# Pooled attention and a GELU MLP on one core: the loads of one group's K and V issued behind a transpose

## The chip, the cores and the metric

The kernel runs on 1 core of one Trainium2 chip. The metric is the device time of one execution in microseconds (us), and the figure quoted is the median of several runs. The profile comes from one execution that the hardware profiler recorded. Its span runs from the first to the last instruction on the core, so it is a little shorter than the time of the run.

The engines are called as in the profile: PE is the matrix engine (PEld its weight loads), DVE the vector engine, ACT the scalar engine, POOL the GpSimd engine. SP is the engine that issues every load, store and transposing DMA of this kernel, in program order.

## The reference

Attention over 8 batches and 8 heads, with 576 queries of 64 elements each. K and V are first averaged over 8 neighbouring rows, so that 72 pooled keys remain per head. An MLP with a tanh GELU follows on the 4608 tokens.

```python
k_p = k.reshape(B, H, S // 8, 8, D).mean(axis=3)      # B, H, S, D = 8, 8, 576, 64
v_p = v.reshape(B, H, S // 8, 8, D).mean(axis=3)
scores = q @ k_p.transpose(0, 1, 3, 2) / np.sqrt(D)
attn = np.exp(scores - scores.max(-1, keepdims=True))
attn = attn / (attn.sum(-1, keepdims=True) + 1e-09)
x = (attn @ v_p).transpose(0, 2, 1, 3).reshape(B * S, H * D)      # 4608 x 512
h = x @ w_in                                                     # w_in 512 x 2048
g = 0.5 * h * (1 + np.tanh(np.sqrt(2 / np.pi) * (h + 0.044715 * h ** 3)))
out = g @ w_out                                                  # w_out 2048 x 512
```

## The kernel before

**Groups and steps.** The tokens are worked on in nine groups of 512. Groups 0 to 7 hold the first 512 queries of each batch; the ninth, called `R`, gathers the last 64 queries of all eight batches. The order is 0 to 6, then `R`, then 7. Each step is the MLP of one group, with the attention of the next group woven into it, and the loads for the group after that. Step 0 is `mlp_first`. The loop from line 727 makes the steps 1 to 8; in step 1 (`n_ == 1`) the MLP is that of group 1, the attention that of group 2 (`n`), and the loads are those of group 3 (`n2`).

**The order by hand.** The schedule is manual: every engine runs its instructions in program order. PE's matmuls of the MLP are counted by slots. The first 64 slots are the hidden layer (`hidden`, line 376: four matmuls for each of 16 rows of blocks, then a GELU on ACT). Slots 64 to 175 are the output layer (line 485: seven products, 16 matmuls each, of which three take sums that `g_sums` makes on DVE). `at(hooks, s, f, ...)` puts the call `f` ahead of the matmul of slot `s`; calls of one slot run in the order of the `at` lines.

**What the slots of step 1 hold.** These matter here:

- Slot 22: `pool`, `dup_k` and `k_transpose_dma` of group 2. DVE averages K, and SP issues the transposing DMA into `kTd` (line 199).
- Slots 28, 32, 36, 40: `cast_q` of group 2 on ACT (line 88), a quarter of the queries each, from `q_sb` into the bf16 tile `q_b`.
- Slot 28 too: `load_kv` of group 3 (lines 667 to 674): a new `kv` tile, then four loads. Those of line 108 carry 1024 KB each (K first and V last), and those of lines 103 and 101 carry 128 KB each.
- Slot 41: `q_transpose_dma` of group 2 (line 220). SP waits for the four casts, then issues one transposing DMA from `q_b` into `qT`.
- Slots 57 and 58: `load_q` of group 3 (line 120, 1024 KB) and two parts of `R`'s queries (line 124, 128 KB each).
- Slots 68, 71, 92 and 100: `scores` on PE (line 229), which reads `qT` and `kbd`, then the exponential on ACT (line 244).
- Slots 81, 97, 104 and 114: `norm` (lines 251, 260, 263) and `e_transpose_dma` (line 293), which SP issues into `eT`.
- Slot 116: `cast_gated`, POOL's cast of group 3's queries.
- Slot 156: the first half of `values_part` (line 348) on PE, which reads the first two of the four `eT` parts. The second half follows in slot 4 of the next step and reads the other two.
- Slot 164: `q_transpose_dma` of group 3.

The later steps have the same slots with two differences: their query transposes were issued in the step before (slot 164), and `pool` and `k_transpose_dma` come in slot 12.

**Buffers.** `kv` and `q_sb` have two buffers each; `qT`, `q_b`, `kTd` and `eT` have one. The `kv` tile of group 3 takes the buffer of group 1, whose last reader on DVE ends at 49.2 us in the profiled run.

Of the kernel before, what the change touches and what calls it, by code (L numbers as in the profile page):

```python
# [19 lines left out]
def kernel(  # L20
# [655 lines left out]
    def at(hooks, s, f, *a):  # L676
        hooks.setdefault(s, []).append(lambda: f(*a))
# [6 lines left out]
    hooks = {}  # L684
# [42 lines left out]
    for n_, g in enumerate(seq):  # L727
        if n_ == 0:
            continue
        hooks = {}  # L730
        if n_ == 1:
            for i in range(1, 4):
                at(hooks, i, w_sums, i, 0, NP, nc.vector)
            at(hooks, 36, g_sums, 0, 4)
        else:
            at(hooks, 20, g_sums, 0, 2)
            at(hooks, 36, g_sums, 2, 4)
        at(hooks, 57, g_sums, 4, 6)
        at(hooks, 65, g_sums, 6, 8)
        if n_ + 1 < len(seq):  # L740
            n = seq[n_ + 1]
            b = B - 1 if n == R else n
            kv = n != B - 1
            if n_ == 1:
                for j in range(4):
                    at(hooks, 28 + 4 * j, cast_q, n, j, j + 1, nc.scalar)
                at(hooks, 41, qT_tile, n)
                at(hooks, 41, q_transpose_dma, n)
            if kv:
                t0 = 22 if n_ == 1 else 12  # L750
                at(hooks, t0, pool, b, 0, 5)
                at(hooks, t0, dup_k, b, 0, 5)
                at(hooks, t0, kT_tile, b, None)
                at(hooks, t0, k_transpose_dma, b)
                t1 = t0 + (16 if n_ == 1 else 24)
                at(hooks, t1, pool, b, 5, 9)
                at(hooks, t1, spread_v, b, nc.gpsimd)
                at(hooks, 56, k_spread, b, [nc.vector, nc.vector])
            for j in range(4):
                sj = 64 + ([4, 4, 30, 34] if n == R else [4, 7, 28, 36])[j]  # L760
                at(hooks, sj, scores, n, j)
                at(hooks, sj, exps, n, j)
                if j == 0:
                    at(hooks, 64 + 17, eT_tile, n)
                nj = 64 + [17, 33, 40, 50][j]
                at(hooks, nj, norm, n, j, nc.gpsimd if j == 1 else nc.vector)
                at(hooks, nj, e_transpose_dma, n, j)
            at(hooks, 64 + 66, nc.scalar.preload_act_table_set, GELU_SET)
            at(hooks, 64 + 92, xT_tile, n)
            at(hooks, 64 + 92, values_part, n, 0, [nc.scalar, nc.vector])  # L770
        if n_ > 1:
            at(hooks, 4, values_part, g, 1, [nc.scalar, nc.vector])
        if n_ + 2 < len(seq):
            n2 = seq[n_ + 2]
            if n2 != R:
                at(hooks, 57, q_tile, n2)
                at(hooks, 57, load_q, n2, 0, 4, nc.sync)
            at(hooks, 64 + 52, cast_gated, n2)
            at(hooks, 64 + 100, qT_tile, n2)
            at(hooks, 64 + 100, q_transpose_dma, n2)  # L780
            at(hooks, 28, load_kv, n2)
        if n_ == 1:
            at(hooks, 58, q_tile, R)
        if 1 <= n_ <= 4:
            at(hooks, 58, load_q, R, n_ - 1, n_, nc.sync)
        mlp(g, hooks, n_ + 1 == len(seq), n_ > 1)
# [30 lines left out]
```

## Time and profile before

| What | Value |
|---|---|
| median of 6 runs | 296.47 us (295.70 to 298.62) |
| the profiled run | 295.7 us |
| its span | 294.0 us |
| PE busy | 279.3 us (95%) |
| DVE, ACT, POOL busy | 206.4, 166.8, 63.6 us |
| DMA | 56.41 MB, mean 192 GB/s |
| mean granted PE clock | 0.987 of full speed |

How to read it: the page gives the busy time of each engine, the span in 40 equal slices (7.35 us each) with a digit for the busy tenths, and the groups of instructions with the idle time ahead of them and what ended it. The chain of waits follows the work that ended last back to the start. The timeline of SP lists its issues with the time that each issue held SP; the time from an issue to the landing of its data is given separately.

### The profile page before, as it was taken

The page shows a single profiled execution, that of the slowest core. Times are in us where ns is not written, and L with a number is a line of the kernel's source. Part 1 is how long each engine was busy: PE and PEld are TensorE (multiplying, and loading weights), DVE is VectorE, ACT ScalarE, POOL GpSimd, SP SyncE. Part 2 cuts the span into 40 slices and gives each one's busy share as a digit, 9 for nine tenths or more (in the row PEclk, how much of TensorE's full clock was granted, in tenths as well). Part 3 has the DMA queues.
Part 4 walks back from the last instruction along what each step waited for, and adds up shares of the span by engine and source line. Part 5 has one row for each costly group of instructions (what it writes and reads, how often), then busy time and mean ns, then how long its engine had stood idle before and what let it go on. Part 6 is the DMA issues. An engine that isn't in the chain of part 4 may idle for free.

```text
span 294.0 us, 5594 instructions
## 1 busy us (share of the span) xinstructions
PE 279.3 (95%) x2203; PEld 199.5 (68%) x2203; DVE 206.4 (70%) x379; ACT 166.8 (57%) x262; POOL 63.6 (22%) x97
## 2 busy tenths in 40 slices
PE   8799999991999999999999999999999999999994
PEld 4578753440887488748874886498648965986583
DVE  4891879985476897689768967895899435944531
ACT  1586584792345674666367636664675467546610
POOL 3575343021040124022302220312031200100000
PEclk9999999998699999999999999999999999999999
DMA  7999999999647797799888949824841560144003
GB/s 230 354 387 337 377 383 183 337 293 312 176 90 214 227 298 91 215 236 294 86 221 256 278 89 223 290 57 110 197 141 26 120 162 2 28 99 108 1 2 144
DMA packets 71419, 56.41 MB, mean 192 GB/s; under 512 B 45664, under 2 KB 55392, under 8 KB 71392
## 3 DMA queue, kind: packets, MB, share of 16 engines
q1 hardware_dynamic: 71392, 56.04, 70.6%
q8 instruction: 17, 0.28, 0.4%
q14 instruction: 10, 0.08, 0.1%
HBM read 36.70 MB, written 9.44 MB: 157 GB/s over the span
## 4 chain that ended last, share of the span: by engine, by line
PE 80%; DMA 11%; DVE 5%; SPq 1%; POOL 1%; issue 0%; DVEq 0%
PE mm L485 31%; PE mm L380 28%; PE mm L391 9%; DMA kv<-in_k_dram 5%; DMA qT<-q_b 4%; PE xo L348 4%; DMA q_sb<-in_q_dram 3%; PE sc L229 2%; PE x L485 2%; DVE eb L263 1%; PE mm L396 1%; DVE kv L147 1%; DVE den L251 1%; DVE kv L148 1%; SPq L108 1%; PE xo L356 1%
## 5 line engine op out<-in xcount | busy, mean ns | idle before, releaser
L380 PE MATMUL mm<-xT,w_in_b 128*128 128x512 bf16 x400 | 87.8, 379 | 0.0
L382 ACT ACTIVATE gT<-mm 128x512 bf16<-128x512 f32 x100 | 59.7, 598 | 25.0 <-PE mm L380 24.9
L380 PEld LDWEIGHTS <-w_in_b 128*128 128x128 bf16 x400 | 39.1, 98 | 45.8 <-issue 0.3
L485 PEld LDWEIGHTS <-gT 128*128 128x128 bf16 x512 | 50.3, 100 | 7.9
L169 POOL TENSOR_TENSOR vbd<-kvb,vmask 128x256 bf16<-128x256 bf16 (+2 forms) x40 | 23.7, 614 | 95.3 <-DVE kvb L149 95.1
L391 PE MATMUL mm<-xT,w_in_b 128*128 128x256 bf16 x352 | 42.2, 273 | 0.2 <-DVE xT L90 0.2
L485 PEld LDWEIGHTS <-stage 128*128 128x128 bf16 x384 | 37.2, 98 | 4.2
L391 PEld LDWEIGHTS <-w_in_b 128*128 128x128 bf16 x352 | 34.0, 98 | 4.2 <-issue 0.3
L393 ACT ACTIVATE gT<-mm 128x512 bf16<-128x512 f32 x44 | 26.2, 597 | 15.6 <-PE mm L391 15.6
L244 ACT ACTIVATE e<-sc 128x576 f32<-128x576 f32 x36 | 22.6, 650 | 19.1 <-PE sc L229 11.1
L485 PE MATMUL mm<-w_out_b,gT 128*128 128x256 bf16 x240 | 32.6, 283 | 0.0
L90 DVE CAST xT<-xo 128x512 bf16<-128x512 f32 x16 | 11.0, 691 | 29.0 <-PE xo L348 24.1
L485 PE MATMUL mm<-tw,gT 128*128 128x256 bf16 x240 | 28.7, 273 | 0.0
L88 ACT COPY osb<-mm 128x512 f32<-128x512 f32 x23 | 13.5, 586 | 26.6 <-PE mm L485 26.6
L251 DVE TENSOR_REDUCE den<-e 128x8 f32<-128x576 f32 x36 | 26.4, 735 | 2.3 <-ACT e L244 2.3
L485 PE MATMUL mm<-tw,stage 128*128 128x256 bf16 x224 | 27.9, 273 | 0.0
L147 DVE TENSOR_TENSOR kv<-kv 128x1024 f32<-128x1024 f32 (+3 forms) x19 | 21.0, 1107 | 7.6 <-DMA kv<-in_k_dram 6.3
L431 DVE TENSOR_TENSOR stage<-gT 128x512 bf16<-128x512 bf16 (+1 forms) x31 | 16.2, 522 | 13.1 <-ACT gT L382 7.8
L88 ACT CAST xT<-xo 128x512 bf16<-128x512 f32 (+1 forms) x18 | 11.3, 633 | 18.4 <-PE xo L348 11.0
L263 DVE TENSOR_TENSOR eb<-e,r 128x576 bf16<-128x576 f32 x24 | 20.3, 847 | 0.8
L229 PE MATMUL sc<-kbd,qT 128*128 128x144 bf16 x128 | 13.8, 232 | 6.9 <-DMA qT<-q_b 6.6
L263 POOL TENSOR_TENSOR eb<-e,r 128x576 bf16<-128x576 f32 x6 | 6.9, 1149 | 60.3 <-ACT e L244 54.5
(86 smaller groups left out, 303.7 us busy)
## 6 DMA issues: line engine op xcount, KB each, us to landing
kv<-in_k_dram SPq DMA_DIRECT2D x7, 1024.0 KB, 6.6
q_sb<-in_q_dram SPq DMA_DIRECT2D x7, 1024.0 KB, 10.6
out_dram<-osb SPq DMA_DIRECT2D x13, 512.0 KB, 3.0
kv<-in_v_dram SPq DMA_DIRECT2D x6, 1024.0 KB, 8.6
kv<-in_v_dram SPq DMA_DIRECT2D x4, 512.0 KB, 10.3
w_in_s<-in_moe_w_in_dram SPq DMA_DIRECT2D x4, 512.0 KB, 9.0
stage<-in_moe_w_in_dram SPq DMA_DIRECT2D x4, 512.0 KB, 11.5
w_out_s<-in_moe_w_out_dram SPq DMA_DIRECT2D x2, 1024.0 KB, 13.4
```

Source lines behind the costliest of these rows:

```text
L88: eng.copy(out=out, in_=in_)
L147: add(out=t[:, :, 0:4, :], in0=t[:, :, 0:4, :], in1=t[:, :, 4:8, :], op=ALU.add)
L169: eng.tensor_tensor(out=vbd[p0:128, b, n0:n1, :].rearrange("p (c r) (hh d) -> p c (r hh) d", c=max(m, 1), d=D), in0=kvb[p0:128, 4 + c0:4 + ...
L229: nc.tensor.matmul(out=o, lhsT=qT[:, j, pr, :], rhs=kbd[:, g, pr].rearrange("d hh s -> d (hh s)"), start=True, stop=True)
L244: nc.scalar.activation(out=e.rearrange("p (x h) s -> p x (h s)", x=2), in_=sc[:, :, 0:4 * Sp], func=ACT.Exp, scale=1.0 / 64.0)
L251: nc.vector.reduce_sum(out=den, in_=e, axis=AX.X)
L263: eng.tensor_tensor(out=o.rearrange("p (h s) -> p h s", s=Sp), in0=e, in1=r.unsqueeze(2).to_broadcast([128, H, Sp]), op=ALU.mult)
L380: nc.tensor.matmul(out=hp, lhsT=w_in_b[:, ko, fo * 128:(fo + 1) * 128], rhs=st[g]["xT"][:, ko, :], start=(i == 0), stop=(i == KO - 1))
L382: nc.scalar.activation(out=gT[:, fo, :], in_=hp, func=ACT.Gelu_apprx_tanh)
L391: nc.tensor.matmul(out=hp[:, f, :], lhsT=w_in_b[:, ko, (fo + f) * 128:(fo + f + 1) * 128], rhs=st[g]["xT"][:, ko, c0:c0 + 256], start=(ko ...
L393: nc.scalar.activation(out=gT[:, fo:fo + 2, c0:c0 + 256], in_=hp, func=ACT.Gelu_apprx_tanh)
L485: nc.tensor.matmul(out=xs[p] if acc is xs else acc[:, p, :], lhsT=lt, rhs=rt, start=bool(fresh and m == 0 and (p == 0 or (last and acc is ...
```

## The change

One number: in step 1 alone, `load_kv` is put in slot 44 in place of slot 28. Its four loads are issued after `q_transpose_dma` of slot 41 instead of before it. In the other steps `load_kv` stays in slot 28.

```diff
@@ -778,7 +778,7 @@
             at(hooks, 64 + 52, cast_gated, n2)
             at(hooks, 64 + 100, qT_tile, n2)
             at(hooks, 64 + 100, q_transpose_dma, n2)
-            at(hooks, 28, load_kv, n2)
+            at(hooks, 44 if n_ == 1 else 28, load_kv, n2)
         if n_ == 1:
             at(hooks, 58, q_tile, R)
         if 1 <= n_ <= 4:
```

## The prediction

> **What bounds the kernel now.** First the page: PE is busy in nine tenths or more of nearly every slice, so only PE's gaps and its clock can be won. Slices 10 and 11 (66.2 to 80.8 us) have a low clock, and line 229 (`scores`) waited 6.6 us for one transfer.
>
> ```profile
> PE   8799999991999999999999999999999999999994
> PEclk9999999998699999999999999999999999999999
> L229 PE MATMUL sc<-kbd,qT 128*128 128x144 bf16 x128 | 13.8, 232 | 6.9 <-DMA qT<-q_b 6.6
> ```
>
> Second, the chain of waits in order of time, around that place and in the next step.
>
> ```profile
> 52.64 10.41 PE mm L380 x48
> 63.05 10.55 DMA qT<-q_b
> 73.61 0.05 issue
> 73.66 0.66 PE sc L229 x4
> ...
> 86.59 0.87 PE xo L348 x8
> ...
> 104.81 0.25 PE sc L229 x4
> ...
> 115.42 0.87 PE xo L348 x8
> ```
>
> PE stands still from 67.04 us (73.66 less 6.62) to 73.66. From the first scores to `values_part` step 1 then takes 86.59 − 73.66 = 12.93 us; step 2 takes 115.42 − 104.81 = 10.61 us for the same matmuls. The 2.32 us between them is the slow clock. So the place holds 6.62 + 2.32 = 8.94 us.
>
> Third, SP's timeline (start, time that SP was held, line): why is `qT` late?
>
> ```profile
> 59.11 1.23 SPq L199 DMA_TRANSPOSE kTd<-kvb  x1
> 60.40 0.73 SPq L108 DMA_DIRECT2D kv<-in_k_dram  x1
> ...
> 62.36 0.59 SPq L108 DMA_DIRECT2D kv<-in_v_dram  x1
> 63.05 8.54 SPq L220 DMA_TRANSPOSE qT<-q_b  x1
> 71.64 0.58 SPq L120 DMA_DIRECT2D q_sb<-in_q_dram  x1
> ...
> 89.32 3.24 SPq L220 DMA_TRANSPOSE qT<-q_b  x1
> ```
>
> Group 3's K and V were issued just ahead of it. V landed 9.5 us after its issue, at 71.9; `qT` took 10.55 us and landed at 73.6. The six other `qT` transposes landed 5.0 (three times), 5.3, 5.9 and 6.8 us after their issue, and held SP for 3.0 to 3.8 us, not 8.54.
>
> Fourth, windows of the same stretch (the last three columns are clock, DMA share and GB/s).
>
> ```profile
> 63.00:64.00 1.00, 1.00 (x6) 0.47 (x5) 0.97 (x2) 0.96 (x2) 0.00 (x0) 1.00 0.90 62
> 64.00:65.00 1.00, 1.00 (x7) 0.47 (x5) 0.93 (x2) 0.69 (x2) 0.00 (x0) 1.00 0.84 207
> 70.80:71.40 0.60, 0.00 (x0) 0.00 (x0) 0.00 (x0) 0.00 (x0) 0.00 (x0) 0.92 1.02 315
> 73.20:73.80 0.60, 0.14 (x2) 0.15 (x3) 0.00 (x0) 0.00 (x0) 0.00 (x0) 0.50 0.47 85
> 78.00:78.60 0.60, 0.60 (x6) 0.54 (x5) 0.60 (x2) 0.00 (x0) 0.00 (x0) 0.89 0.26 43
> 78.60:79.20 0.60, 0.60 (x10) 0.56 (x9) 0.53 (x3) 0.00 (x0) 0.00 (x0) 1.00 0.00 0
> ```
>
> They cut the traffic into parts. `kTd` (landed at 65.3) takes the low rate up to about 64.3. K and V move from 64.3 to 71.3 (7.0 us), `qT` to 73.5 (2.2 us), the query loads to 78.1 (some 4.5 us). The DMA is then idle until SP issues the first `eT` at 79.84.
>
> **The change, part by part.**
>
> *Issue of `qT`.* SP waits for the last cast, which ends on ACT at 62.34 + 0.64 = 62.98 us. Before, SP was through with V at 62.95; so the issue stays at 63.05. It now holds SP for about 3.2 us (3.0 to 3.8 in the undisturbed rows) instead of 8.54. Nothing else is behind it on SP but loads.
>
> *Landing of `qT`.* Only `kTd` is ahead, busy to 64.3. Undisturbed landings of 5.0 to 6.8 us give 68.05 to 69.85. I take 5.5, a little over their mean because of `kTd`: 68.55. PE needs it at 67.04, so the scores start at 68.6 and 1.6 us of the stall stay; 5.1 us go.
>
> *The clock.* The row: idle from 67.04, the clock fell at about 71.3 (0.92 in 70.8 to 71.4), 4.3 us on, and was back at 78.1. [...]
>
> *The four loads.* They are issued from about 66.35 instead of 60.40 and held SP for 2.4 us together: until 68.9, and the query loads follow at once (before: 71.64). Their data come behind `qT`'s, from about 68.4. [...] For K and V themselves it costs nothing: DVE first reads group 3's K at 92.04, and 68.4 + 7.0 = 75.4 is far ahead, even with that read some 5 us earlier. [...] The cost lies with the transfers behind them.
>
> *What is late next: `eT`.* Loads of 3.67 MB (2 × 1024, 2 × 128, 1024 and 2 × 128 KB) are in front of the `eT` transposes. They took 7.0 + 4.5 = 11.5 us in step 1; in step 2 they moved from about 98.2 to 109.0 (10.8). With 11.2, they end at 68.4 + 11.2 = 79.6 instead of 78.1. But `values_part` now wants the first two `eT` at 68.6 + 10.61 = 79.2 instead of 86.59. That is a new stall. For its size nothing in the trace fits exactly, so two ends. If both `eT` (5 blocks each) already stand in the queue, they need 10/16 of `qT`'s 2.2 us and 0.3 us to land: 79.6 + 1.7 = 81.3. If SP is held until the loads have moved, as `qT` held it until 71.59, then the first issue ends at 79.9, the second takes 1.2 us and lands 1.4 us after its issue (the undisturbed 2.6 less 1.2): 82.5. I take the middle, 81.9: a stall of 2.7 us, too short for the clock.
>
> *Behind it.* The third and fourth `eT` take 2 × 1.25 us of issue after the second, and the second half of `values_part` comes 3.06 us after the first (89.65 − 86.59): just in time. Group 3's queries land near 80, and POOL's cast, 84.40 before and gated by the fourth `norm`, comes at about 79.5 to 80. Its query transpose follows at 84 to 85 and is wanted at about 100. From there every step is as before: step 1's `values_part` to step 2's is 28.83 us, step 2's to step 3's 144.25 − 115.42 = 28.83.
>
> **Sum.** `values_part` of step 1 starts at 81.9 + 0.1 = 82.0 instead of 86.59: 4.6 us less. In terms: −5.1 of stall, −2.3 of clock, +2.8 of the new wait. The profiled run of 295.7 becomes 291.1. It is the fastest of six; set against the median, 296.47 − 4.6 = 291.9 us.
>
> **Rivals.** A change of 0.5% (1.5 us) is about what the measurement can tell from none.
>
> *The new wait doesn't arise* (10%). The `eT` transposes find a gap, or the loads move at the 390 GB/s of their best windows: 3.67/0.39 = 9.4 us, end at 77.8. With `qT` after 5.0 us the gain is 8.94 − 1.1 = 7.8: 288.7 us. For it: the DMA idled before `eT` in the run before. Against: 390 GB/s was never held for 3.67 MB; 10.8 us is the best seen.
>
> *The new wait is long* (12%). `qT` at 69.85, loads from 69.6 in 11.5 us, `eT` held and its landing stretched by 1 us (the first `eT` of steps 2 to 4 took 4.4, 3.6 and 4.2 us): 81.1 + 2.9 + 1 = 85.0. Gain 1.5 without a fall of the clock, none or −0.8 with it: 295 to 297.
>
> *Slower* (4%). One mechanism: K and V, then the queries, crawl in front of `eT` with scores, exponentials and PE back at full load. At 68 to 69 us, K and V moved at 236 GB/s. Were all 3.67 MB that slow, 15.6 us, they would end at 84.0 and the second `eT` land at 86.9, 7.7 us after it is wanted; the clock falls too (2.3): 86.9 − 86.59 + 2.3 = 2.6 slower, 299.1 us. It decides from a landing at about 84.3 on with the clock fallen (85.8 for a loss over 1.5 us). Against: the same loads took 10.8 us in step 2 with PE at full load.
>
> *It doesn't do what it says* (2%). `qT` was slow through stores and `kTd` ahead, not through K and V: 296.5 us. The stores of step 0 landed by 65.0 and `kTd` at 65.3, which leaves 8.3 us to V and `qT`.
>
> **How the numbers follow.** The forecast has 72%; within it `qT`'s 5.0 to 6.8 us and the two ends for `eT` give gains of about 3 to 6: 290.5 to 293.5. The range reaches to the rivals on both sides, 289.2 to 294.6. Faster by over 0.5%: 72 + 10 and half of the long wait, 88%. Within 0.5%: 7%. Slower: 5%.
>
> **What would show it.** In the new profile: the `qT` issue of 63.05 holds SP for 3 to 4 us and lands at 68 to 70; the wait of line 229 is 1 to 3 us; the clock stays at 1.00 from 66 to 80; K is issued at about 66.4; a new wait of line 348 for `eT` of 1.5 to 4 us at about 79 to 82; all later steps are 28.8 us. I am wrong if line 348 waits over 4 us, if the clock falls there, or if `qT` lands after 70.

## The result and the profile after

The changed kernel takes 295.12 us (median of 34 runs, 293.45 to 296.62) against 296.52 us of the kernel before in all its runs (71, 294.79 to 298.62). The ratio is 0.9958, with a 95% interval of 0.9944 to 0.9971: 0.4% faster, 1.4 us where 4.6 were forecast. The profiled run took 295.35 us with a span of 293.6 us.

First the page of the changed kernel. The rows of the two waits have changed places.

```profile
PE   8879999999669999999999999999999999999994
PEclk9999999999959999999999999999999999999999
L348 PE MATMUL xo<-eT,vbd 128*128 128x256 bf16 x96 | 13.3, 284 | 5.2 <-DMA eT<-eb 5.2
```

Line 229 no longer stands among the costly groups with a wait for `qT`; line 348 now waits 5.2 us for `eT`. The low clock has moved from slices 10 and 11 to slice 12. Next, the changed kernel's chain of waits in order of time (start, us, what).

```profile
63.02 4.30 DMA qT<-q_b
67.32 0.05 issue
67.37 0.42 PE sc L229 x4
...
72.04 4.82 PE mm L485 x44
76.86 1.94 SPq L293
...
78.90 4.29 DMA eT<-eb
83.19 0.14 issue
83.33 1.87 PE xo L348 x8
85.19 4.11 PE mm L485 x20
...
93.66 10.36 PE mm L380 x48
```

PE waits for the second of the four `eT` parts, since line 348 reads the first two. `qT` lands 4.3 us after its issue instead of 10.55, and the scores start at 67.37 instead of 73.66: 6.3 us earlier. Then PE stands still from 78.16 to 83.33. After that the 8 matmuls of line 348 take 1.87 us (0.87 before) and the 20 behind them 4.11 us (2.18 before): the clock is halved (0.50 in a row of the windows below). From the first `values_part` to the 48 matmuls of step 2's hidden layer (line 380) it is 93.66 − 83.33 = 10.33 us, before 94.02 − 86.59 = 7.43. The new wait thus costs 5.17 us and 2.9 us of clock, and of the 6.3 + 2.3 = 8.6 us that were won only 94.02 − 93.66 = 0.36 us are left in this pair of profiles: 0.2 us went into the first scores (0.42 us in place of 0.25). The profiled run of the kernel before was 0.8 us faster than its median, so the pair shows less than the medians do. The steps from 2 on are 28.83 us, as before.

SP's timeline of the changed kernel shows why `eT` is late (start, time SP was held, line):

```profile
63.02 2.45 SPq L220 DMA_TRANSPOSE qT<-q_b  x1
65.52 0.58 SPq L108 DMA_DIRECT2D kv<-in_k_dram  x1
...
67.37 0.59 SPq L108 DMA_DIRECT2D kv<-in_v_dram  x1
68.00 0.64 SPq L120 DMA_DIRECT2D q_sb<-in_q_dram  x1
68.68 4.93 SPq L124 DMA_DIRECT2D q_r<-in_q_dram  x2
73.72 9.39 SPq L293 DMA_TRANSPOSE eT<-eb  x4
```

The four `eT` hold SP for 9.39 us (5.99 before). The first alone holds it for 5.08 us and lands 8.4 us after its issue; the second is issued at 78.90 and lands 4.3 us later, at 83.2. Half-microsecond windows of the same run (the last three columns are clock, DMA share and GB/s; a share can exceed 1, because a packet's whole time is counted in the window in which it begins):

```profile
77.50:78.00 0.50, 0.50 (x6) 0.34 (x4) 0.50 (x2) 0.00 (x0) 0.00 (x0) 1.00 1.25 288
79.50:80.00 0.50, 0.00 (x0) 0.00 (x0) 0.00 (x0) 0.00 (x0) 0.00 (x0) 1.00 1.77 58
80.50:81.00 0.50, 0.00 (x0) 0.00 (x0) 0.00 (x0) 0.00 (x0) 0.28 (x1) 1.00 0.08 16
81.50:82.00 0.50, 0.00 (x0) 0.00 (x0) 0.00 (x0) 0.00 (x0) 0.50 (x2) 1.00 1.28 283
82.00:82.50 0.50, 0.00 (x0) 0.00 (x0) 0.00 (x0) 0.00 (x0) 0.50 (x1) 0.67 1.26 284
83.50:84.00 0.50, 0.50 (x4) 0.38 (x3) 0.00 (x0) 0.00 (x0) 0.00 (x0) 0.50 0.94 180
```

From 79.5 almost nothing moves for 2 us (58 GB/s in 79.5 to 80.0, 16 in 80.5 to 81.0), and only from 81.5 do the `eT` data come (283 GB/s). In 82.0 to 82.5 the clock falls (0.67 on average, 0.50 behind it). The loads in front are not through when the rate drops. Group 3's queries land at 80.6, where POOL's cast of them can start, and the two loads of `R`'s queries, issued at 68.7 and 71.9, take 12.3 and 9.6 us and land at 81.0 and 81.5 (a row of POOL's timeline, then two of the view of `q_r`):

```profile
80.72 2.02 POOL L90 CAST q_b<-q_sb 128x1024 bf16<-128x1024 f32 x2 [3.40 <-DMA q_sb<-in_q_dram]
L124 SPq DMA_DIRECT2D q_r<-in_q_dram x2: 1712/2442/3172, 68.7 to 71.9; - x2
DMA to landing us min/median/max: 9.6/11.0/12.3
```

### The profile page after: what moved, and what is told of

It reads as the page before. It is cut to its first block, busy times and chain, and to the rows that moved or that the text cites. A ratio compares the mean times of both kernels' runs of the same rounds, so it can differ in the third digit from the quotient of the medians.

```text
span 293.6 us, 5594 instructions
## 1 busy us (share of the span) xinstructions
PE 280.0 (95%) x2203; PEld 199.8 (68%) x2203; DVE 207.0 (71%) x379; ACT 166.7 (57%) x262; POOL 63.0 (21%) x97
## 4 chain that ended last, share of the span: by engine, by line
PE 87%; DVE 7%; DMA 3%; SPq 1%; issue 0%; POOL 0%; ACT 0%; POOLq 0%
PE mm L485 31%; PE mm L380 28%; PE mm L391 12%; PE xo L348 4%; PE x L485 2%; PE sc L229 2%; PE warm L591 2%; DVE den L251 2%; DMA qT<-q_b 1%; DMA eT<-eb 1%; DVE eb L263 1%; PE mm L396 1%; PE vp L156 1%; SPq L293 1%; PE xo L356 1%; DVE kv L147 1%
## 5 line engine op out<-in xcount | busy, mean ns | idle before, releaser
L485 PE MATMUL mm<-w_out_b,gT 128*128 128x256 bf16 x240 | 30.8, 273 | 0.0
L485 PE MATMUL mm<-tw,gT 128*128 128x256 bf16 x240 | 30.2, 282 | 0.0
L432 DVE TENSOR_TENSOR gT<-gT 128x512 bf16<-128x512 bf16 (+1 forms) x31 | 14.8, 477 | 6.6 <-ACT gT L382 5.1
L348 PE MATMUL xo<-eT,vbd 128*128 128x256 bf16 x96 | 13.3, 284 | 5.2 <-DMA eT<-eb 5.2
```

The source lines that it names most:

```text
L348: nc.tensor.matmul(out=xo[pr // 2][:, x, :], lhsT=vbd[:, g, n, :], rhs=eT[:, 2 * half:2 * half + 2, c, :], start=(y == 0), stop=(y == 1))
L485: nc.tensor.matmul(out=xs[p] if acc is xs else acc[:, p, :], lhsT=lt, rhs=rt, start=bool(fresh and m == 0 and (p == 0 or (last and acc is ...
```

## The experiments

Each is an edit of the changed kernel, save where it says otherwise. The ratios are to the kernel before, run on the same chip. They are what to compare: the experiments ran on three chips, and the kernel before has medians of 295.38 to 296.83 us there.

**1. K and V behind `eT`.**

```diff
-            at(hooks, 44 if n_ == 1 else 28, load_kv, n2)
+            at(hooks, 115 if n_ == 1 else 28, load_kv, n2)
```

> In step 1 load_kv goes to slot 115, behind the four eT transposes, in place of slot 44. Theory (the gain was given back because the eT transposes stand behind 3.67 MB of loads, and the wait of 5.2 us then halves the clock for another 2.9 us): line 348 no longer waits for eT in step 1, the clock stays full after 60 us, and the time falls by about 8 us from the changed kernel's 295.1, to 287. Rival (the loads cannot be hidden anywhere near there): K and V come too late for step 2 or hold up group 3's query transpose behind them, a new wait of line 229 or line 147 takes the place, and the time stays at 292 or more.

Measured: 291.31 us, ratio 0.984 (0.978 to 0.990). In step 1 there was no wait for `eT`, as the theory has it. But 287 was missed: step 2 got a wait of line 348 for `eT` of 1.8 us. The rival was right that the wait moves, and wrong about the line. DVE pools K and the 128 KB piece of V (line 101) at the start of step 2, and they were there only at 85.5. So `kTd` and the loads behind it came late as measured from PE, and in the chain of this run stands:

```profile
79.69 5.80 DMA kv<-in_v_dram
85.61 1.50 DVE kv L147
...
104.84 4.72 DMA eT<-eb
```

**2. The query loads behind `eT`.** The `at` lines of slots 57 and 58 get `115 if n_ == 1 else ...`.

> load_kv stays in slot 44; the query loads of step 1 (group 3's and R's first part, 1.3 MB) go from slots 57 and 58 to slot 115, behind the eT transposes. Theory (the amount of data ahead of eT sets the new wait): only K and V are ahead, 7 us of data from about 68, so the second eT lands at 77.5 to 78.7 where PE wants it at 78.2; the wait is 0 to 0.5 us, no fall of the clock, time 287 to 288. Rival (a transposing DMA behind any running load starts some 2 to 3 us late): the second eT lands at 79.5 to 80.5, a wait of 1.3 to 2.3 us without a fall of the clock, time 288.5 to 289.5.

Measured: 291.30 us, ratio 0.987 (0.981 to 0.992). Step 1 again has no wait. The chain of this run shows where the gain went; 78.08 is step 1's `values_part`, the rest is step 2.

```profile
78.08 0.87 PE xo L348 x8
...
96.31 0.25 PE sc L229 x4
...
104.85 4.94 DMA eT<-eb
109.79 0.09 issue
109.88 1.03 PE xo L348 x8
```

Step 2 takes 109.88 − 78.08 = 31.8 us instead of 28.8. SP's timeline of this run says why: the transpose of group 3's queries had to wait for queries loaded late, and it held up everything behind it.

```profile
88.05 1.81 SPq L220 DMA_TRANSPOSE qT<-q_b  x1
...
91.18 1.45 SPq L199 DMA_TRANSPOSE kTd<-kvb  x1
92.67 0.65 SPq L108 DMA_DIRECT2D kv<-in_k_dram  x1
```

Step 2's K was issued 96.31 − 92.67 = 3.6 us ahead of its scores; before, it was 104.81 − 96.49 = 8.3 us. The loads were late relative to PE here too; in step 1 of the changed kernel K is issued 67.37 − 65.52 = 1.85 us ahead of the scores.

**3. Only R's part behind `eT`.** The two loads of 128 KB go from slot 58 to slot 115.

> Only R's first part (two loads of 128 KB in rows of 256 bytes) goes behind the eT transposes; K, V and group 3's queries stay ahead of them. In the changed kernel the DMA moved 16 to 71 GB/s between 80 and 81.5 us, after the loads had slowed and before the eT data came. Theory of bytes: 0.26 MB less at 290 GB/s is 0.9 us; eT's second part lands at 82.3, the wait is 4.3 us, the clock may still fall; time 292 to 294.5. Theory of small pieces (the pause comes from the tail of the short-row loads): the pause goes, the second eT lands near 80, the wait is under 2 us, the clock stays full; time 288 to 289.5.

Measured: 291.69 us, ratio 0.986 (0.981 to 0.991). Neither theory holds as it stood. The chain:

```profile
74.72 6.52 DMA eT<-eb
81.24 0.14 issue
81.37 1.87 PE xo L348 x8
83.24 2.82 PE mm L485 x20
```

The second `eT` landed at 81.2, 2.0 us earlier, which is twice what the bytes explain. The stretch with almost no traffic stayed (36 GB/s or less from 78.5 to 79.5), so it does not come from R's part alone. The wait was 3.2 us, and that still halved the clock (0.50), for 3.4 us.

**4. Keep PE busy in the wait.**

```diff
+            if n_ == 1:
+                at(hooks, 64 + 92, warm_up, 20, "sc")
             at(hooks, 64 + 92, values_part, n, 0, [nc.scalar, nc.vector])
```

> The changed kernel with 20 matmuls of zeros (128x512) put into PE's program of step 1 just ahead of slot 156's values_part; they take 20 x 0.216 = 4.3 us of the 5.2 us in which PE waits for eT, and nothing reads them. Theory (2.9 us of what was given back are the clock, halved by the idle wait): the clock stays at 1.00 from 66 to 95 us and the time falls to about 292.2. Rival (the clock's fall costs little, or falls all the same): 295, or more if the matmuls come on top of the wait.

Measured: 292.55 us, ratio 0.989 (0.985 to 0.994), which lies apart from the changed kernel's interval. The second `eT` came as late as ever (83.4), but the clock stayed (mean 1.000 in the profiled run):

```profile
79.04 4.34 DMA eT<-eb
83.38 0.14 issue
83.51 1.03 PE xo L348 x8
84.55 2.18 PE mm L485 x20
```

The same matmuls take 1.03 and 2.18 us in place of 1.87 and 4.11. The fall of the clock is worth 1.9 us by the ratios (0.9958 less 0.9893) and 2.6 by the medians (which are not of the same chips); the profile has 2.9.

**5 and 6. V behind `eT`; then also R's parts one step later.**

```diff
+            if n_ == 1:
+                at(hooks, 115, load_main, n2, "v", 0, 4, nc.sync)   # load_kv(3) in slot 44 without it
...
-        if 1 <= n_ <= 4:                                            # only in the sixth
-            at(hooks, 58, load_q, R, n_ - 1, n_, nc.sync)
+        if 2 <= n_ <= 5:
+            at(hooks, 58, load_q, R, n_ - 2, n_ - 1, nc.sync)
```

> The changed kernel, but group 3's V load of 1024 KB goes from slot 44 to slot 115, behind the eT transposes; K and the two halves stay in slot 44. Theory (the data ahead of eT set the wait): 1.05 MB at 300 GB/s less is 3.5 us; the second eT lands near 79.7 instead of 83.2, PE wants it at 78.1, a wait of 1 to 2 us, the clock stays full; 295.1 less 3.5 less 2.9 is 288.7, say 288 to 290. Rival (any load that is moved back only moves the wait): step 2 gets a new wait for its eT of 2 us or more, as the two runs before it had, and the time is 291 or more.

> As the run before, and R's four parts are loaded in steps 2 to 5 instead of 1 to 4 (0.26 MB less ahead of eT in step 1). Theory: the second eT lands another 1 to 2 us earlier, at 78 to 78.7, a wait under 0.6 us in step 1, the time 1 us under the run before: 287 to 289. Rival (the wait comes back in step 2, whose loads are untouched): no better than the run before.

Measured: 289.66 us, ratio 0.976 (0.973 to 0.980), and 288.23 us, ratio 0.971 (0.968 to 0.974). In the fifth run the second `eT` landed at 80.9, later than the 79.7 expected, with a wait of 2.7 us that left the clock alone in the profiled run (1.00 in 76 to 90 us). In the sixth it landed at 78.0 and PE did not wait at all; its chain has no transfer after `qT`:

```profile
63.27 4.29 DMA qT<-q_b
...
72.26 6.11 PE mm L485 x56
78.38 0.87 PE xo L348 x8
...
107.20 0.87 PE xo L348 x8
```

Step 2 is 107.20 − 78.38 = 28.82 us: nothing came back. V is needed latest of group 3's data (DVE pools it from slot 36 of step 2, K from slot 12), so it can be moved without holding up `kTd` or the query transpose. This is the fastest version found, 2.9% under the kernel before.

**7. Half the change: V alone behind the transpose.** K and the two loads of 128 KB stay in slot 28; V goes to slot 44.

> Half the change: K and the two halves stay in slot 28 ahead of the transpose of the queries, V alone goes to slot 44 behind it. The same bytes are ahead of eT. Theory (the backlog sets when eT lands, near 83 in any order, and the length of each single wait sets the clock): qT lands near 70.3, a wait of 3.2 us, then a wait of some 2 us for eT; neither halves the clock, and the time is 2.9 us under the changed kernel, 292.2. Rival (what counts is the sum of waits, not how they are cut): 295, as the changed kernel.

Measured: 294.22 us, ratio 0.990 (0.986 to 0.993).

```profile
63.83 7.32 DMA qT<-q_b
71.20 0.66 PE sc L229 x4
...
78.70 6.11 PE mm L485 x56
84.81 0.87 PE xo L348 x8
```

`qT` came at 71.15, and the one wait of 4.2 us halved the clock (0.50 from 70.3 to 77.0), against the expectation. The second `eT` landed at 82.5 (79.5 plus 3.0), and PE, later by then, did not wait for it. That is near the 83.2 of the changed kernel, but not for one cause alone: here POOL finished the source of this transpose only at 79.5 (its timeline),

```profile
78.36 1.15 POOL L263 TENSOR_TENSOR eb<-e,r 128x576 bf16<-128x576 f32 x1 [10.59 <-ACT e L244]
```

and it landed only 0.4 us over the 2.6 us of an undisturbed one. What the two orders do share is the queue in front: the last load landed at 81.3 here (71.0 plus 10.3) and at 81.5 in the changed kernel. The order sets whether PE waits before the scores or after them, and with that how much is lost. Half the change gains more than the whole, by the ratios (the intervals lie apart) and in the profiles: the 48 matmuls of step 2's hidden layer start at 92.23 instead of 93.66. It pays 4.2 us of wait and 3.0 of clock, the whole change 0.3 and 5.2 of waits, 2.9 of clock and 0.2 in the first scores.

**8. The kernel before, kept busy in its wait.**

```diff
+            if n_ == 1:
+                at(hooks, 68, warm_up, 28, "sc")
             for j in range(4):
```

> The kernel before with 28 matmuls of zeros (128x512, 6.0 us) ahead of slot 68's scores in step 1, inside the 6.6 us in which PE waits for qT. Theory (the clock's fall in the wait costs 2.3 us): the clock stays at 1.00 from 66 to 80 us and the time is 294.2, so that change and before differ by about 1 to 1.7 us once neither loses the clock. Rival (the clock in the wait costs nothing): 296.5.

Measured: 294.77 us, ratio 0.992 (0.988 to 0.995); the clock was 1.00 from 66 to 90 us. The lower clock in the wait for `qT` was worth 0.8%, 2.5 us. In the run profiled here `qT` landed at 75.4 (63.58 plus 11.83), 1.8 us later than in the profile of before: that wait differs from run to run. Experiments 4 and 8 show change and before with little loss of clock in either: 0.989 and 0.992. Their intervals overlap, so nothing that can be told apart is left of the change then.

**9 and 10. What made R's part dear.** The sixth kernel plus one load of 256 KB in slot 58 that nothing reads, to 128 partitions, in rows of 2 KB and of 256 bytes.

```diff
+            extra = stage[:, 3072:3584].rearrange("p (x d) -> p x d", d=D)
+            at(hooks, 58, lambda e=extra: nc.sync.dma_start(out=e, in_=rows(k, 0)[0:128]))
```

(The tenth has `in_=q[0, :, 0:128].rearrange("h t d -> t h d")`.)

> The sixth experiment's kernel plus one load of 256 KB in rows of 2 KB (a piece of K into an unused part of stage, which nothing reads), issued in slot 58 of step 1, where R's part stood. It asks whether R's 0.26 MB were dear for their bytes or for their short rows. Theory of bytes: as dear as R's part was in the fifth experiment, the second eT lands near 80.9 and the time is 1.4 us above the sixth (288.2): 289.6. Theory of short rows: only 0.26 MB at 300 GB/s = 0.9 us, the second eT lands at 78.5 to 79.3, the time is 0 to 0.9 us above: 288.2 to 289.1.

> As the run before, but the 256 KB come in rows of 256 bytes (1024 rows of group 0's queries, to all 128 partitions; nothing reads them). Theory of short rows: the second eT lands near 80 to 81 as with R's part, and the time is 289.2 to 290. Theory of bytes: the same as the run with long rows. If the rows don't matter and R's part is dear for going to 64 partitions in two transfers, both runs are near 288.5.

Measured: 288.54 us, ratio 0.975 (0.969 to 0.981), and 289.30 us, ratio 0.976 (0.971 to 0.980). The second `eT` landed at 78.9 and at 79.4, against 78.0 without the load and 80.9 with R's part (experiment 5). In these profiles, one each, the bytes cost 0.9 us and short rows 0.5 us more; the other 1.5 us of R's part are neither. What is left are its two transfers and its 64 partitions each; those two were not taken apart. The times cannot tell 9, 10 and 5 from each other: their intervals overlap.

## Why the prediction was wrong

*What bounded the kernel* was right, and experiment 8 bears out the clock's share: 2.3 us forecast, 2.5 measured.

*Issue and landing of `qT`*: issue at 63.02 (63.05 forecast). The landing was mis-sized the harmless way: 67.3 for 68.55, with 4.3 us where the rows of before gave 5.0 to 6.8. The stall that stays is 0.3 us for 1.6. That 1.6 us there would leave the clock at full speed, on which the −2.3 of the sum rests, was the author's estimate and no run shows it; with 0.3 us the clock was 1.00 from 66 to 82 us.

*The four loads*: issued at 65.5 (66.35 forecast), and K and V, landed by 76.7, cost nothing themselves. The cost fell on what was queued behind them, as that step said: the second `eT` landed at 83.2.

*What is late next* is the step that failed. Place and mechanism were right: line 348 waits for the second `eT`, in slot 156. The term was mis-sized: 2.7 us forecast, 5.17 measured. Both ends of the difference were off. PE wanted `eT` at 78.16 instead of 79.2, because `qT` was better than forecast; and `eT` landed at 83.2 instead of 81.9, beyond even the upper end of 82.5. Most of this second error is the time of the 3.67 MB in front, which was put too short. In the kernel before the last of these loads landed at 79.1, 1.0 us after the 78.1 that was read as their end; the 79.6 of the forecast thus stands for a landing at 80.6, and it came at 81.5. From there to the second `eT` it was 1.7 us, where the forecast left 1.3. Why the loads took longer is not shown. The time of step 2, 10.8 us to 109.0, had been read too short in the same way. These two rows follow that end, and the last load landed at 110.7:

```profile
109.00:109.50 0.50, 0.50 (x9) 0.47 (x7) 0.50 (x2) 0.11 (x1) 0.00 (x0) 1.00 0.90 125
109.50:110.00 0.50, 0.50 (x7) 0.46 (x5) 0.47 (x2) 0.50 (x1) 0.00 (x0) 1.00 0.32 39
```

The trace of before also had a standstill like that of 79.5 to 81.5 in small (62 GB/s in 63 to 64 us, ahead of `kTd`), and it was read as the slow rate of a transpose. The three `eT` landings of 3.6 to 4.4 us in steps 2 to 4 were put into a rival only.

*"Too short for the clock"* fell with it, and that was the larger half: the 2.3 us won at the first wait were paid back as 2.9 at the second. Experiment 4 shows this part by itself. The forecast gave a fall of the clock only to the rival of the long wait, at 12%, and the outcome is that rival's: 295 to 297 forecast, 295.12 measured, with `qT` early rather than late. The range ended at 294.6.

*The sum*: −5.1 −2.3 +2.8 was forecast; the profiles show −6.3 −2.3 +5.2 +2.9 and 0.2 of the first scores, which is −0.3 (−0.36 between the traces).

*The rivals*: a wait that doesn't arise did not happen with this order (with V and R's parts moved it did, experiment 6). The slower case did not happen: the loads had landed by 81.5, where it had them end at 84.0. That the change does not do what it says is ruled out by `qT` at 67.3.

What the forecast lacked was a plainer view: the bytes in front of the last transpose are the same before and after the change. The last load in front landed at 81.5 in the changed kernel and at 81.3 in experiments 7 (V alone moved) and 8 (the order of before); in the profile of before it was 79.1. The second `eT` landed 2 us or more earlier only where bytes went behind it (77.2 in experiments 1 and 2; 81.2, 80.9 and 78.0 in 3, 5 and 6), and only bytes that nothing needs soon (V, R's part) keep step 2 whole.

## What to carry to other kernels

When a transfer is late because others are queued ahead, expect that changing the order moves the wait to the next transfer of the same queue, as it did here (from 6.6 us for `qT` to 5.2 for `eT`): follow every later one against the time at which it will then be wanted, and look for bytes that can leave the stretch, not only for a better order within it. Treat a wait as a difference of two estimates whose errors add: here 1.0 us early and 1.3 us late doubled it. And ask of each wait that remains whether it halves the PE clock: here that cost 2.3 us behind the wait of 6.6 and 2.9 behind that of 5.2.

## What the hardware showed unexpectedly

**Packets of the transposes that stand still.** From 79.5 to 81.5 us the changed kernel moved 16 to 71 GB/s, although `eT` had been issued at 73.72. The packet records of its trace show that the DMA was not idle: 23 packets of 256 bytes begin between 79.29 and 80.04 us and all end between 81.38 and 81.42, just ahead of the last landing of a load (81.5). Experiment 6 (48 and 27 GB/s in 75.5 to 76.0 and 76.0 to 76.5), whose loads come in pieces of 1 KB or more, shows that such packets are `eT`'s: 21 of them begin from 75.05 us on and all end between 76.64 and 76.69, 0.2 us before group 3's queries land. Experiments 3, 5, 7, 9 and 10 have the same picture, 0.15 to 0.2 us before the last load lands (20 GB/s in 78.9 to 79.2 in experiment 3, 16 in 78.0 to 78.5 in 5, at most 3 in 79.8 to 80.0 in 7, 19 and 18 in 77.0 to 77.5 in 9 and 10). But it is no rule that the last load ends it: in step 2 of the kernel before, 20 packets end together at 112.8, 2 us after that landing (110.7). And between V and `qT` in the kernel before nothing stood (290 GB/s in 71.4 to 72.0). What holds these packets is open.

**When the clock falls.** It fell 4.3 us (before), 4.0 (after), 3.2 (experiment 7) and 2.9 us (experiment 3) after PE's last matmul (the ends of matmuls in the trace are modelled), so the four falls have no time in common. From fall to return it is 6.8 us in three of them and 3.4 in experiment 3. The wait of 2.7 us in experiment 5 left the clock at 1.00 in the profiled run. What decides between these is not shown. The mean clock was 0.982 to 0.992 in every run of the changed kernel, against 0.997 to 1.000 in those of experiment 4, which keeps PE busy. The 4.3 us of the one fall in the profile of before, which the prediction went by, made a lost clock look rarer than it is.
